# Attention with routed experts on one core: routed rows leave PSUM by VectorE, and a prep of q stands behind the routing step

## The chip, the cores and the metric

The kernel runs on one core of a Trainium2 chip. TensorE (PE) multiplies, its weight loads are listed apart (PEld); VectorE (DVE), ScalarE (ACT) and GpSimd (POOL) compute; SyncE (SP) issues transfers. The metric is the device time of one execution in microseconds (us), lower is better.

## The reference

Attention over 8 batches, 8 heads, 576 positions and 64 dimensions, with a bias from a small network, and then a mixture of 8 experts in which each of the 4608 tokens goes to one expert:

```python
scores = scale * np.matmul(q, k.transpose(0, 1, 3, 2))
...
h = np.maximum(x @ w1 + b1, 0.0)
bias = h @ w2
scores = scores + bias.transpose(2, 0, 1)[None, :, :, :]
scores = scores - np.max(scores, axis=-1, keepdims=True)
attn = np.exp(scores)
attn = attn / (np.sum(attn, axis=-1, keepdims=True) + 1e-09)
return np.matmul(attn, v).astype(np.float32)
...
logits = x @ w_gate + modality_bias[modality_id]
e_idx = np.argmax(logits, axis=1)
...
for e in range(E):
    mask = e_idx == e
    h = np.maximum(x[mask] @ w1[e], 0.0)
    out[mask] = gate_w[mask, None] * (h @ w2[e])
```

Here x is the attention's output with the heads side by side, 4608 rows of 512, and gate_w is the softmax weight of the chosen expert.

## The kernel before, in words

First a table of biases is built (to about 72 us), then attention runs over 32 pairs of heads, n = 0 to 31, four pairs to a batch, and last come expert tiles of 256 routed rows. Attention and the routing of the batch before are interleaved by a list written out by hand, `ORDER` (L572): each pair has five units, u = 0 to 4, and each letter of a unit's string is one operation, emitted in that order. Each engine runs its own instructions in the order in which they were emitted.

The letters that matter here: S is one slot of scores (L415), on TensorE, followed by a reduction on VectorE (L445) that reads PSUM, adds the bias and finds the row's extreme; e and f are the exponentials of the unit's slots on ScalarE (L459). T and t transpose a chunk of exponentials (L473) into the banks eps1 and eps0, from which ScalarE or VectorE copies it to eT. R is rtrans (L495), which transposes the remainders into a bank of xps, copied to rT by ScalarE. The digits 0 to 4 are parts of prep (L368) of the next pair: four transposes into a bank of xps (L379), scaled into QT by VectorE (L319) or copied into KT. W issues the transfers that swap QT's halves. a and b are av (L504), the product with v, through xps as well. X and B take the next step of the routing of the batch before from a list (`route_steps`, L730), if what it needs has been done; D stores finished rows to memory.

Two banks of PSUM, xps0 and xps1, serve all of R, prep, av and the routing steps. `xbank` (L306) hands them out in turn, so each user waits until what was put there two uses before has been copied out. The copies go through `take` (L312), which gives a copy to ScalarE where its name is in `ON_ACT` (L310), and to VectorE otherwise.

A batch's routing steps with kind X are the logits (two parts, L758), their transposes, the ranks (L833), and five row steps (`s_rows`, L854): TensorE transposes 128 tokens of the attention's output back into rows (L859), the rows are copied to one of two buffers (xrb) that take turns, GpSimd scales them (L866), appends the gate (L869), and D stores them (L902). For batches 0 to 6 row steps 0 and 1 fall in unit 4 of the pairs 6, 10, ..., 30, row step 2 in unit 0 of the pairs 7, 11, ..., 31, and steps 3 and 4 in unit 4 of those; the second part of the logits falls in unit 0 of pairs 5, 9, ..., 29. In the other units 0 the X finds nothing to do. The last batch's steps run beside the first expert tiles, and their rows go to buffers in the space of NBm.

```python
def xbank(self):
    self.n_x += 1
    return self.xps[self.n_x % 2]
...
self.take("xr", xr[0:n, 0:DM], ps[0:n, :])
```

Of the kernel before, what the change touches and what calls it, by code (L numbers as in the profile page):

```python
# [22 lines left out]
S = 576  # L23
# [84 lines left out]
class Attn:  # L108
# [198 lines left out]
        self.n_x += 1  # L307
        return self.xps[self.n_x % 2]

    ON_ACT = ("av0", "av1", "e00", "e11", "e21", "e30", "e31", "e40", "e41", "prep2", "prep5", "rT", "xr", "lt0")  # L310

    def take(self, what, out, ps, scale=1.0):  # L312

        if what in self.ON_ACT:
            self.nc.scalar.activation(out, ps, AF.Copy, scale=scale)  # L315
# [213 lines left out]
    def first_steps(self, route):  # L529
# [40 lines left out]


    ORDER = (  # L572
# [893 lines left out]
```

## Time and profile before

| | |
|---|---|
| median of 3 runs | 1157.64 us (1157.51 to 1159.23) |
| profiled execution | 1149.1 us |
| its span, first to last instruction | 1147.3 us |
| TensorE busy | 1098.1 us, 96% of the span |
| VectorE busy | 739.5 us, 64% |
| ScalarE busy | 730.8 us, 64% |
| GpSimd busy | 359.7 us, 31% |
| mean granted TensorE clock | 0.994 |

The time of the profiled execution includes a little before the first and behind the last instruction, 1.8 us together. Rows of the trace hold the start, the duration, the engine, the line, the operation, what it writes and reads, and in brackets how long the engine was idle before it and what ended that. A row with x4 merges four instructions that stand together. TensorE's matmuls overlap, so a row's duration is not the pace of its instructions; the starts of the weight loads show that better.

### The profile page before, as it was taken

What the parts mean: (1) busy time and instruction counts of PE and PEld (TensorE: products, weight loads), DVE (VectorE), ACT (ScalarE), POOL (GpSimd) and SP (SyncE); (2) the same over time, 40 slices, a digit from 0 to 9 for tenths busy, and PEclk for the clock granted to TensorE, in tenths of its full rate; (3) what the DMA queues carried; (4) which work ended last, traced back from release to release, by engine and by line L of the source; (5) the groups of instructions that cost most, each with busy time, mean ns of one, the idle gap of its engine ahead of it and who ended that gap; (6) DMA issues with size and microseconds to landing.
All of it is one profiled execution on the core that took longest, in us unless ns stands there. A gap on an engine that the chain in (4) does not pass through costs nothing. (4 is left out here: it accounts for less than half of the span.)

```text
span 1147.3 us, 22992 instructions
## 1 busy us (share of the span) xinstructions
PE 1098.1 (96%) x8202; PEld 917.0 (80%) x8202; DVE 739.5 (64%) x1548; ACT 730.8 (64%) x1428; POOL 359.7 (31%) x514
## 2 busy tenths in 40 slices
PE   7979999999999999999999899999999999999997
PEld 3458877778788778887777779899998999999975
DVE  8965667676585766766767457675565556645576
ACT  7767767667767767676766666445564555545566
POOL 0013324434435344254443234412112212222121
PEclk9989999999999999999999999999999999999999
DMA  6984434754636445355464611212115115111370
GB/s 175 222 186 110 113 94 121 113 119 109 127 96 132 116 125 115 98 127 116 113 124 108 195 33 66 52 46 65 38 38 194 56 47 203 46 43 60 112 268 22
DMA packets 91456, 124.54 MB, mean 109 GB/s; under 512 B 35713, under 2 KB 60673, under 8 KB 91332
## 3 DMA queue, kind: packets, MB, share of 16 engines
q1 hardware_dynamic: 83236, 101.61, 36.0%
q0 software_dynamic: 8000, 21.35, 6.1%
q8 instruction: 68, 1.11, 0.5%
q14 instruction: 56, 0.46, 0.2%
q10 hardware_dynamic: 96, 0.00, 0.0%
HBM read 140.36 MB, written 19.90 MB: 140 GB/s over the span
## 5 line engine op out<-in xcount | busy, mean ns | idle before, releaser
L459 ACT ACTIVATE Eb<-Eb,mn 128x576 f32<-128x576 f32 x288 | 221.9, 773 | 82.2 <-DVE mn L445 82.1
L445 DVE CUSTOM_DVE_ANT_0 Eb<-sps,NBm 128x576 f32<-128x576 f32 x256 | 185.7, 753 | 104.7 <-ACT eT L315 78.5
L430 PE MATMUL sps<-KT,QT 128*128 128x288 f32 x1152 | 202.7, 310 | 11.5 <-DMA QT<-QT 8.0
L430 PEld LDWEIGHTS sps<-KT,QT 128*128 128x128 f32 x1152 | 160.5, 190 | 21.3 <-issue 7.9
L1181 PE MATMUL p<-QT,w1hi 128*128 128x256 f32 x1152 | 162.1, 283 | 1.6 <-ACT w1hi L1154 1.6
L1181 PEld LDWEIGHTS p<-QT,w1hi 128*128 128x128 f32 x1152 | 149.4, 192 | 3.9 <-ACT w1hi L1154 2.5
L473 PE MATMUL eps<-idf,Eb 128*128 128x128 f32 x1024 | 146.0, 276 | 3.4 <-DVE eT L317 2.9
L1207 POOL DMA_INDIRECT out<-mo,idt x36 | 48.1, 1336 | 297.7 <-ACT mo L1206 261.2
L1184 DVE SCALAR_TENSOR_TENSOR hl<-p,hh 128x512 fp32r<-128x512 f32 x72 | 49.7, 690 | 139.9 <-ACT hh L1183 139.9
L515 PE MATMUL xps<-eT,vraw 128*64 128x288 f32 x1024 | 137.8, 411 | 1.1 <-DVE QT L319 0.5
L464 POOL COPY rem<-Eb 128x128 f32<-128x128 f32 x128 | 37.1, 289 | 302.3 <-ACT Eb L459 301.3
L473 PEld LDWEIGHTS eps<-idf,Eb 128*128 128x128 f32 x1024 | 118.5, 142 | 16.2 <-DVE eT L317 4.9
L315 ACT ACTIVATE eT<-eps 128x512 f32<-128x512 f32 x192 | 110.6, 592 | 32.3 <-PE eps L473 28.5
L1148 DVE TENSOR_TENSOR w2lo<-NBm,w2hi 128x1024 fp32r<-128x1024 f32 x84 | 102.4, 1225 | 24.9 <-ACT w2hi L1147 24.9
L1198 PE MATMUL p<-w2hi,hh 128*128 128x512 f32 x288 | 114.2, 396 | 0.0
L1183 ACT ACTIVATE hh<-p 128x512 fp32r<-128x512 f32 x72 | 43.0, 597 | 110.7 <-PE p L1181 100.4
L1198 PE MATMUL p<-w2hi,hl 128*128 128x512 f32 x288 | 112.5, 391 | 0.0
L317 DVE COPY eT<-eps 128x512 f32<-128x512 f32 x96 | 65.9, 686 | 61.1 <-ACT xTb L315 54.1
L515 PEld LDWEIGHTS xps<-eT,vraw 128*64 128x64 f32 x1024 | 67.9, 136 | 46.0 <-issue 5.3
L1148 DVE TENSOR_TENSOR w1lo<-NBm,w1hi 128x1024 fp32r<-128x1024 f32 x84 | 97.7, 1225 | 0.2 <-ACT w1hi L1147 0.2
L1181 PE MATMUL p<-QT,w1lo 128*128 128x256 f32 x576 | 92.8, 283 | 0.2 <-DVE w1lo L1155 0.2
L1147 ACT CAST w2hi<-NBm 128x1024 fp32r<-128x1024 f32 x84 | 86.8, 1041 | 0.7 <-ACTq L1311 0.7
(233 smaller groups left out, 1907.8 us busy)
## 6 DMA issues: line engine op xcount, KB each, us to landing
NBm<-moe_w SPq DMA_DIRECT2D x24, 2048.0 KB
NBm<-moe_w SPq DMA_DIRECT2D x46, 1024.0 KB
QT<-QT SPq DMA_DIRECT2D x64, 304.0 KB
NBm<-xTb SPq DMA_DIRECT2D x32, 288.0 KB
KH<-KT SPq DMA_DIRECT2D x64, 144.0 KB
qraw<-q SPq DMA_DIRECT2D x32, 256.0 KB
kraw<-k SPq DMA_DIRECT2D x32, 256.0 KB
vraw<-v SPq DMA_DIRECT2D x32, 256.0 KB
```

Of the source, the lines that this page charges most:

```text
L315: self.nc.scalar.activation(out, ps, AF.Copy, scale=scale)
L317: self.nc.vector.tensor_copy(out, ps)
L430: nc.tensor.matmul(ps[:, half, :], q, k[:, HS * half : HS * half + HS], start=i == 0, stop=i == len(terms) - 1, skip_group_check=True,)
L445: nc.vector.tensor_tensor_reduce(out=e.rearrange("p (t w) -> p t w", t=2), in0=ps, in1=nb.rearrange("p (t w) -> p t w", t=2), scale=1.0, s ...
L459: self.nc.scalar.activation(e, e, AF.Exp, bias=mn, scale=-1.0, accum_out=sm)
L473: nc.tensor.transpose(ps[:, k, :], e[:, part, P * k : P * k + P], self.idf)
L515: nc.tensor.matmul(ps[o, :], v[:, h, k, :], self.eT[:, h, k, sl], start=k == 0, stop=False, tile_position=(0, 64 * h), skip_group_check=True,)
L1147: self.nc.scalar.copy(h, w)
L1148: self.nc.vector.tensor_tensor(l, w, h.bitcast(F32), op=ALU.subtract)
L1181: nc.tensor.matmul(ps[:, a, :], w[:, c, fs], x[:, c, :], start=i == 0, stop=i == len(ops) - 1)
L1184: nc.vector.scalar_tensor_tensor(hl[:, sl, :], ps, 0.0, hh[:, sl, :].bitcast(F32), op0=ALU.max, op1=ALU.subtract)
L1198: nc.tensor.matmul(ps, h[:, f, sl], m[:, f, :], start=i == 0, stop=i == len(ops) - 1)
```

## The change

The name xr leaves the list of copies that ScalarE does: the five row copies of each batch, 40 in all, go to VectorE. And in unit 0 the prep part 0 moves from before X to behind f; as e and f are work of ScalarE alone, the prep then stands behind the routing step on TensorE and VectorE.

```diff
-    ON_ACT = ("av0", "av1", "e00", "e11", "e21", "e30", "e31", "e40", "e41", "prep2", "prep5", "rT", "xr", "lt0")
+    ON_ACT = ("av0", "av1", "e00", "e11", "e21", "e30", "e31", "e40", "e41", "prep2", "prep5", "rT", "lt0")
...
-        "S S T t R 0 X e f C Z L",
+        "S S T t R X e f 0 C Z L",
```

On TensorE in unit 0 of pair 15, with row step 2 (L859), prep part 0 (the first L379) and, in unit 1, prep part 1 (the last line); xps_77 and xps_78 are the two banks, and L501 is rtrans:

```order
 L501 MATMUL xps_78<-idf,rem_2_3863 128x128
 L501 MATMUL xps_78<-idf,rem_3_3904 128x128
-L379 MATMUL xps_77<-idr,qs 128x128 x4
-L859 MATMUL xps_78<-idf,xTb_94 128x128 x4
+L859 MATMUL xps_77<-idf,xTb_94 128x128 x4
+L379 MATMUL xps_78<-idr,qs 128x128 x4
 L430 MATMUL sps_736<-KT_108,QT_73 128x288 x4
 L379 MATMUL xps_77<-idr,qs 128x128 x4
```

Row step 2 and prep part 0 change places and banks; prep part 1 keeps its bank, in which row step 2 now stands before it instead of prep part 0.

On VectorE from the end of pair 14 to unit 0 of pair 15; eT<-eps_738 is e20, L847 and L849 belong to the positions, L445 with mn_0 and mn_1 are the reductions of slots 0 and 1, and QT is prep part 0:

```order
 L841 TENSOR_TENSOR rks_3926<-rks_3926,oh 128x40
+L317 COPY xrb_90<-xps_78 128x512
 L317 COPY eT<-eps_738 128x4x128
 L847 TENSOR_REDUCE pf_3948<-rks_3926 128x5
 L849 CAST pos_3950<-pf_3948 128x5
+L317 COPY xrb_89<-xps_77 128x512
 L445 ISA Eb,mn_0_3966<-sps_736,NBm 128x576
 L445 ISA mn_0_3966 128x1
 L445 ISA Eb,mn_1_3972<-sps_737,NBm 128x576
 L445 ISA mn_1_3972 128x1
```

Two row copies enter the queue ahead of the reductions of slots 0 and 1. Right behind these the third one enters, ahead of the scaling of prep part 0:

```order
-L319 TENSOR_SCALAR QT_72<-xps_77 128x512
+L317 COPY xrb_90<-xps_77 128x512
+L319 TENSOR_SCALAR QT_72<-xps_78 128x512
 L445 ISA Eb,mn_2_4018<-sps_736,NBm 128x576
```

It writes the same buffer, xrb_90, as the first of the three.

On TensorE in unit 0 of pair 13, with the second part of the logits (L767):

```order
 L501 MATMUL xps_78<-idf,rem_2_3423 128x128
 L501 MATMUL xps_78<-idf,rem_3_3465 128x128
-L379 MATMUL xps_77<-idr,qs 128x128 x4
-L767 MATMUL xps_78<-xTb_94,wgb 32x64 x4
+L767 MATMUL xps_77<-xTb_94,wgb 32x64 x4
+L379 MATMUL xps_78<-idr,qs 128x128 x4
```

Logits and prep change places and banks in the same way. The orders of GpSimd and SyncE are as before.

## Rows read from the trace of the kernel before

**Rows 1.** The page's totals: busy time of each engine, its share of the span, its instructions.

```profile
PE 1098.1 (96%) x8202; PEld 917.0 (80%) x8202; DVE 739.5 (64%) x1548; ACT 730.8 (64%) x1428; POOL 359.7 (31%) x514
```

**Rows 2.** Busy time of each engine in the attention stretch: the stretch and its length, busy time and instructions of each engine, then the granted clock, the transfers' share and GB/s.

```profile
90.00:670.00 580.00, 560.49 (x4528) 456.98 (x4525) 373.04 (x1006) 406.17 (x979) 240.12 (x390) 1.00 0.52 118
```

**Rows 3.** What TensorE waited for between 88 and 670 us: the line that waited, the releaser, total us, times, longest.

```profile
PE sps L430 <- DMA QT<-QT: 4.8, 4, 2.7
PE xps L767 <- ACT rT L315: 3.5, 7, 0.5
PE sps L430 <- DVE mn L445: 3.2, 8, 0.5
PE xps L859 <- ACT rT L315: 3.0, 6, 0.5
```

**Rows 4.** Two groups of copies out of PSUM over the whole span: busy us, mean ns of one, idle before.

```profile
L317 DVE COPY eT<-eps 128x512 f32<-128x512 f32 x96 | 65.9, 686 | 61.1 <-ACT xTb L315 54.1 <-PE eps L473 5.3 <-PE sps L430 1.4
...
L315 ACT ACTIVATE xrb<-xps 128x512 f32<-128x512 f32 (+1 forms) x42 | 24.3, 594 | 10.7 <-PE xps L379 4.9 <-DMA xg<-xrb 4.3 <-PE sps L430 1.0
```

**Rows 5.** Instructions in order of time, end of pair 14 and begin of pair 15: the copies of row steps 0 and 1 on ScalarE, VectorE's work, the two groups of transposes of unit 0 on TensorE, and the first scaling of rows on GpSimd.

```profile
338.61 0.60 ACT L315 ACTIVATE xrb<-xps 128x512 f32<-128x512 f32 x1
...
339.56 0.68 DVE L317 COPY eT<-eps 128x512 f32<-128x512 f32 x1
...
340.16 0.18 DVE L847 TENSOR_REDUCE pf<-rks 128x5 f32<-128x40 f32 x1
340.34 0.60 ACT L315 ACTIVATE xrb<-xps 128x512 f32<-128x512 f32 x1
340.37 0.75 DVE L849 CAST pos<-pf 128x5 int32<-128x5 f32 x1
...
340.78 1.04 PE L473 MATMUL eps<-idf,Eb 128*128 128x128 f32 x8
341.03 0.74 DVE L445 CUSTOM_DVE_ANT_0 Eb<-sps,NBm 128x576 f32<-128x576 f32 x1
...
341.05 1.04 POOL L866 TENSOR_TENSOR xrb<-xrb,rec 128x512 f32<-128x512 f32 x1
...
341.70 0.75 DVE L445 CUSTOM_DVE_ANT_0 Eb<-sps,NBm 128x576 f32<-128x576 f32 x1
```

**Rows 6.** The same list a little later, units 0 and 1 of pair 15: rtrans (L501), prep part 0 (L379), the stores of rows (SPq L902, issue), rT, row step 2 (L859), scores of slot 2, prep part 1, the copy of row step 2, and the first av (L515).

```profile
341.65 0.60 PE L501 MATMUL xps<-idf,rem 128*128 128x128 f32 x4
...
341.98 0.42 PEld L379 LDWEIGHTS xps<-idr,qs 128*128 128x128 f32 x4
...
342.25 1.47 SPq L902 DMA_DIRECT2D xg<-xrb  x2
342.39 0.60 ACT L315 ACTIVATE rT<-xps 128x512 f32<-128x512 f32 x1
...
343.04 0.66 PE L859 MATMUL xps<-idf,xTb 128*128 128x128 f32 x4 [0.50 <-ACT rT L315]
343.43 0.57 PEld L430 LDWEIGHTS sps<-KT,QT 128*128 128x128 f32 x4
...
343.94 0.44 PEld L379 LDWEIGHTS xps<-idr,qs 128*128 128x128 f32 x4
...
344.38 0.76 DVE L445 CUSTOM_DVE_ANT_0 Eb<-sps,NBm 128x576 f32<-128x576 f32 x1 [1.05 <-PE sps L430]
344.39 0.60 ACT L315 ACTIVATE xrb<-xps 128x512 f32<-128x512 f32 x1 [1.40 <-DMA xg<-xrb]
...
345.07 0.69 DVE L319 TENSOR_SCALAR QT<-xps 128x512 fp32r<-128x512 f32 x1
...
345.67 0.75 DVE L445 CUSTOM_DVE_ANT_0 Eb<-sps,NBm 128x576 f32<-128x576 f32 x1
345.81 1.65 PEld L515 LDWEIGHTS xps<-eT,vraw 128*64 128x64 f32 x16
```

**Rows 7.** Prep part 1 (L379) and the copy of row step 2 in the first and the last of the six pairs 7, 11, 15, 19, 23 and 27, in order of time.

```profile
195.07 0.44 PEld L379 LDWEIGHTS xps<-idr,qs 128*128 128x128 f32 x4
...
195.58 0.60 ACT L315 ACTIVATE xrb<-xps 128x512 f32<-128x512 f32 x1 [1.46 <-DMA xg<-xrb]
...
566.42 0.44 PEld L379 LDWEIGHTS xps<-idr,qs 128*128 128x128 f32 x4
...
567.19 0.60 ACT L315 ACTIVATE xrb<-xps 128x512 f32<-128x512 f32 x1 [1.71 <-PE xps L379]
```

**Rows 8.** Weight loads in order of time: the second part of the logits (L767) and the scores behind it in pair 13, then prep part 0 and the scores behind it in pair 16, where no routing step stands between.

```profile
305.73 0.16 PEld L767 LDWEIGHTS xps<-xTb,wgb 128*32 128x32 f32 x8 [0.64 <-ACT rT L315]
...
305.98 0.56 PEld L430 LDWEIGHTS sps<-KT,QT 128*128 128x128 f32 x4
...
360.60 0.42 PEld L379 LDWEIGHTS xps<-idr,qs 128*128 128x128 f32 x4
360.97 0.56 PEld L430 LDWEIGHTS sps<-KT,QT 128*128 128x128 f32 x4
```

**Rows 9.** The last batch's rows beside an expert tile: splits of the weights on VectorE, and the transposes of row step 3.

```profile
712.10 1.23 DVE L1148 TENSOR_TENSOR w2lo<-NBm,w2hi 128x1024 fp32r<-128x1024 f32 x1 [0.25 <-ACT w2hi L1147]
...
713.52 5.19 DVE L1148 TENSOR_TENSOR w1lo<-NBm,w1hi 128x1024 fp32r<-128x1024 f32 x4 [0.20 <-ACT w1hi L1147]
...
719.37 0.66 PE L859 MATMUL xps<-idf,xTb 128*128 128x128 f32 x4 [2.16 <-DVE QT L1166]
```

## The prediction

> **What bounds the kernel now.** I read the totals first, then the busy time of the attention stretch, then the list of TensorE's waits there, and last the order of time around one place where the change acts. The totals show TensorE busy for 96% of the span, VectorE and ScalarE for 64% each [rows 1]. In the attention stretch, 90 to 670 us, TensorE is busy 560.49 of 580.00 us at a granted clock of 1.00, the 2.4 GHz level, with VectorE at 373.04 and ScalarE at 406.17 [rows 2]. So TensorE sets the pace there, and neither a freed ScalarE nor a fuller VectorE counts unless it moves a TensorE wait. The waits are few: 3.5 us in 7 pieces before the logits (L767) and 3.0 us in 6 pieces before the row transposes (L859), each on the copy of rT by ScalarE; the rest is smaller pieces and transfers of QT [rows 3]. These 13 pieces of 0.50 us stand exactly in the units 0 that the change reorders: the prep of q, then the routing step, which needs the bank that rtrans has just filled.
>
> **The change part by part.** Pair 15 stands for the six places of rows (pairs 7, 11, 15, 19, 23, 27; pair 31 prepares no next pair). The banks alternate: rtrans fills one (I call it B), the next user takes the other (A), the one after that B again.
>
> *Row steps 0 and 1, unit 4 of pairs 6, 10, ...* Their copies leave ScalarE (0.59 us each) and enter VectorE's queue at 0.69 us each, a row of the same shape and kind [rows 4]; one VectorE copy puts the next start back by 0.60 (339.56 to 340.16). Copy 0 takes the start at 339.56, e20 goes to 340.16, the two position steps to 340.76 and 340.97, copy 1 to 341.63 (340.37 to 341.03 is 0.66), and the reduction of slot 0 from 341.03 to 342.23, that of slot 1 from 341.70 to 342.90 [rows 5]. Who waits? The transposes that refill e20's bank are the second half of a group from 340.78 to 341.82, so they start near 341.3, and e20 now ends at 340.85: covered. GpSimd scales row 0 only at 341.05, copy 0 ends at 340.25: covered, and the store of row 0 is issued at 342.25 as now [rows 5, 6]. If that cover were gone, the cost would be up to the 0.60 of a copy for each, 3.6 us over six places. ScalarE's gain is worth nothing: rT starts at 342.39 because rtrans ends at about 342.25, not because ScalarE is busy [rows 6].
>
> *The swap in pair 15.* Now row step 2 comes first. Its bank A is the one of row step 1, whose copy ends on VectorE at 341.63+0.69 = 342.32; with 0.05 to pass on (rT ends at 342.99, its waiter starts at 343.04) the transposes start at 342.37 instead of 343.04 [rows 6]. But prep of q needs bank B, so it is the one that waits for rT until 343.04, and the scores of unit 1 follow 0.37 behind its start (360.60 to 360.97 in a unit without routing step [rows 8]): 343.41, against 343.43 now. The wait of 0.50 is handed on, not removed: 0.0 us. The scores' bank is free by then (slot 0's reduction, 0.74 long, ends at 342.97).
>
> *What becomes late next.* Prep part 1 in unit 1 takes bank A, from which row 2 must be copied. Before the change that bank had held prep part 0, and row 2 lay in B, which is needed only three steps later. Row 2's copy writes the buffer that row 0 is being stored from: ScalarE starts it at 344.39, although its transposes ran from 343.04 to 343.70; the store was issued at 342.25, so it is free 2.14 us after the issue [rows 6]. VectorE will be free at about 343.66, stand before the same store until 344.39, and hand bank A over at 344.39+0.69+0.05 = 345.13. Prep part 1 starts at 343.94 today [rows 6]: 1.19 us late, with nothing else for TensorE to do, since its queue is in program order. In the first of the six places the copy starts 0.51 behind prep part 1, in the last 0.77 [rows 7]; over the six the mean is 0.585. So 6 x (0.585+0.69+0.05) = 7.95 us. From below, if VectorE need not wait for the store: copy at 343.70, bank free at 344.44, 0.50 us each, 3.0 us. From above, if VectorE's lateness is passed on whole (its next four items all stand behind the copy): 1.19+0.7 each, some 11.5. I take 7.95, since all six rows show the copy starting after the transposes by the same margin, and VectorE meets the same store.
>
> The Trainium skill's page "DMA: Bandwidth & Descriptors" (section on the anatomy of one DMA, given for transfers issued by GpSimd) puts a transfer at about 2.0 us fixed plus its bytes over 436 GB/s, and says the fixed part is mostly the confirmation of the write. For 128 rows of 2064 bytes that is an estimate of 2.6 us, against the 2.14 us here; by it each of the six waits would be 0.46 longer and the sum 12.3 instead of 9.5. The trace decides for 2.14, and both speak against placing this copy ahead of what VectorE owes TensorE.
>
> *Behind it.* On VectorE the copy is followed by the scaling of prep 0 (344.99), slot 2's reduction (345.59) and the scaling of prep 1 (346.28 to 346.97; spacings 0.60 and 0.69 from 345.07 to 345.67 and 344.38 to 345.07 [rows 6]). The first av of unit 1 takes that bank; it starts at 345.81 now, 347.00 with the shift, and may start at 347.02. I take 0.05 each, 0.3 us; bounds 0 and 0.35.
>
> *The logits units (pairs 5, 9, ..., 29: seven).* Here too the wait for rT is handed on to the prep. Now the scores follow the logits' start by 0.25 (305.73 to 305.98), then the prep's by 0.37 [rows 8]: 7 x 0.12 = 0.84 us lost. Bounds: 0 to 7 x 0.25.
>
> *Row steps 3 and 4* stand side by side in unit 4 of pairs 7, 11, ... and put two copies before e20. The scores and the first transposes of the next unit lie between them and the next use of their banks and of e20's. I take nothing; where that cover fails it is up to one copy each, 0.60 x 7 = 4.2 us.
>
> *The last batch's five rows* are prepared beside the expert tiles. One TensorE wait there, 2.16 us at 719.37, is on VectorE, which runs four weight splits of 5.19 us from 713.52 right before it [rows 9]; row 2's copy now stands ahead of these splits and puts them back by 0.41, as the split before it ends at about 713.3. 0.41 us; bounds 0 and 3 (five copies, each 0.60).
>
> Sum: 7.95 + 0.3 + 0.84 + 0.41 = 9.5 us. The profiled execution took 1149.1 us (span 1147.3), the median of the runs is 1157.64, 8.5 higher; I add the sum to the median: 1167.1 us.
>
> **The rivals.** *Faster:* the 13 waits of 0.50 us simply go, 6.5 us, 1151.1 us. That needs row 2's copy to be over before prep part 1 comes at 343.94, so the store would have to be done by 343.2, 0.95 us after its issue; and something other than rT's bank for the prep. The rows speak against both. Chance 0.10. *A small loss:* the store does not hold VectorE up (the lower bound): 3.0+0.84+0.41 = 4.3 us, 1161.9 us. For it: ScalarE's late start is put down to TensorE in the last of the six places [rows 7]. Chance 0.08. *No change:* what TensorE loses comes back at waits further down, such as the 4.8 us for QT transfers [rows 3], and the split copy is hidden more than I see: within 2.3 us of 1157.6. Against it: those transfers are issued behind the same preps and move along. Chance 0.07. *A cascade:* VectorE, already late, passes delay on into the next units: 11.5+0.84+0.41 = 12.8 us, 1170.4 us. Against it: VectorE idles 1.05 us before slot 2's reduction [rows 6], and the av of 2 us hides the rest. Chance 0.05.
>
> **How the numbers follow.** The forecast has 0.70. A measurement of this kernel tells about 0.2%, 2.3 us, from no change. Faster: 0.10. Within: 0.07 of the no-change case and 0.02 of the forecast's lower tail, 0.09. Slower: 0.81. The forecast's own range is 1163.5 to 1171; the range given, 1160 to 1172, takes in the small loss and the cascade and leaves out the first and third rival.
>
> **What would show it.** Right: no wait of row transposes or logits on rT, but waits of the preps (L379) in units 0 of the same pairs on rT; in unit 1 of pairs 7, 11, ... prep part 1 waiting some 1.2 us on VectorE, whose copy of row 2 waits for the store; six times. The reductions of slot 0 behind two row copies start about 1.2 us later without a TensorE wait. Wrong: prep part 1 without a wait, a copy that starts straight behind its transposes, or new waits in the transposes that follow e20.

## The result, and the profile after

The change makes the kernel slower: 1164.61 us (median of 7 runs, 1161.85 to 1167.86) against 1153.05 us for the kernel before on the same chip (7 runs, 1145.91 to 1159.23). The ratio is 1.0097 with a 95% interval of 1.0072 to 1.0123, that is 11.2 us of 1153, between 8.3 and 14.2. The forecast was a loss of 9.5 us. The profiled execution of the new kernel took 1161.85 us, its span is 1159.7.

First the totals and the attention stretch of the changed kernel, the views of [rows 1] and [rows 2]; the stretch is 10 us longer here, because attention ends later.

```profile
PE 1102.8 (95%) x8202; PEld 917.6 (79%) x8202; DVE 759.5 (65%) x1588; ACT 713.2 (62%) x1388; POOL 360.0 (31%) x514
```

```profile
90.00:680.00 590.00, 563.16 (x4523) 456.75 (x4519) 390.20 (x1041) 391.18 (x943) 239.67 (x390) 1.00 0.49 116
```

VectorE has 40 instructions more and 20.0 us more work, ScalarE 40 fewer and 17.6 us less. The instruction counts of TensorE are the same and its granted clock in the stretch is 1.00 as before, the 2.4 GHz level. What has grown is TensorE's idle time in the stretch: 19.5 us of 580 before, 26.8 us of 590 now. The list of its waits between 88 and 685 us says which waits these are, the view of [rows 3].

```profile
PE xps L379 <- DVE xrb L317: 6.4, 6, 1.2
PE xps L379 <- ACT rT L315: 5.9, 13, 0.5
PE sps L430 <- DMA QT<-QT: 4.3, 3, 2.9
PE sps L430 <- DVE mn L445: 3.8, 9, 0.6
...
PE xps L515 <- DVE QT L319: 2.7, 2, 1.9
```

The logits (L767) and the row transposes (L859) no longer wait for rT. The prep of q (L379) waits for it in their place, in the same 13 units: 5.9 us, against 3.5 and 3.0 in [rows 3]. And the first line is new: six waits of a prep for a bank that VectorE's copy of a row (xrb, L317) still holds. The weight loads of the same matmuls come earlier in TensorE's queue and show more of each wait:

```profile
PEld xps L379 <- ACT rT L315: 8.5, 13, 0.7
PEld xps L379 <- DVE xrb L317: 7.8, 6, 1.4
```

Six waits, 7.8 us, 1.3 each. Pair 15 of the changed kernel in order of time, the place of [rows 5] and [rows 6]:

```profile
344.27 0.68 DVE L317 COPY xrb<-xps 128x512 f32<-128x512 f32 x1
...
345.76 0.68 DVE L317 COPY xrb<-xps 128x512 f32<-128x512 f32 x1
...
346.81 0.60 PE L859 MATMUL xps<-idf,xTb 128*128 128x128 f32 x4
...
346.97 1.48 SPq L902 DMA_DIRECT2D xg<-xrb  x2
...
347.11 0.60 ACT L315 ACTIVATE rT<-xps 128x512 f32<-128x512 f32 x1
...
347.76 0.39 PEld L379 LDWEIGHTS xps<-idr,qs 128*128 128x128 f32 x4 [0.59 <-ACT rT L315]
...
348.10 0.56 PEld L430 LDWEIGHTS sps<-KT,QT 128*128 128x128 f32 x4
...
349.13 0.69 DVE L317 COPY xrb<-xps 128x512 f32<-128x512 f32 x1 [1.33 <-DMA xg<-xrb]
349.74 0.68 DVE L319 TENSOR_SCALAR QT<-xps 128x512 fp32r<-128x512 f32 x1
349.88 0.40 PEld L379 LDWEIGHTS xps<-idr,qs 128*128 128x128 f32 x4 [1.22 <-DVE xrb L317]
...
351.75 1.65 PEld L515 LDWEIGHTS xps<-eT,vraw 128*64 128x64 f32 x16
```

Read it backwards from the first av (L515) at 351.75. Prep part 1 starts at 349.88, 1.22 us after TensorE was ready for it, because the copy of row step 2 has to empty its bank. That copy starts only at 349.13, although its transposes began at 346.81: it writes the buffer from which row 0 is being stored, and VectorE stood 1.33 us before that store. The store was issued at 346.97, 2.16 us before the copy. All this stands 4.72 us later than in [rows 6] by rT (342.39 there, 347.11 here); the copy by 4.74, the av by 5.94. So the unit is 1.22 us longer, all of it at this one wait.

The length of a batch shows the same without any list. One wait of TensorE comes back once in each batch of four pairs: the one for VectorE's minimum, 0.4 us long, before the scores (L430). From one such wait to the next, in batches without a wait for a transfer, first before and then after the change:

```profile
250.00 0.80 PE L430 MATMUL sps<-KT,QT 128*128 128x288 f32 x4 [0.40 <-DVE mn L445]
...
323.80 0.81 PE L430 MATMUL sps<-KT,QT 128*128 128x288 f32 x4 [0.41 <-DVE mn L445]
```

```profile
404.39 0.80 PE L430 MATMUL sps<-KT,QT 128*128 128x288 f32 x4 [0.41 <-DVE mn L445]
...
479.66 0.81 PE L430 MATMUL sps<-KT,QT 128*128 128x288 f32 x4 [0.39 <-DVE mn L445]
```

73.80 us before, 75.27 after: 1.47 us for each batch. The forecast's terms give 7.95/6 = 1.33 for prep part 1, 0.05 for the av and 0.12 for the logits, together 1.50. I use this batch length below: in most batches without other waits it repeats within about 0.05 us, where whole runs scatter by 6 to 13 us. It is not the same everywhere: another batch before the change (397.59 to 471.76) takes 74.17, because there the av in pair 19 waits 0.39 us for the scaling of prep part 1; against that one the difference is 1.10.

Last, the expert tile of [rows 9], the first row transposes behind the four splits:

```profile
730.00 0.66 PE L859 MATMUL xps<-idf,xTb 128*128 128x128 f32 x4 [2.70 <-DVE QT L1166]
```

2.70 us against 2.16: 0.54 lost, where 0.41 was forecast. Behind this wait the granted clock differs too, three microseconds of each kernel in the view of [rows 2], first after the change and then before:

```profile
731.50:734.50 3.00, 3.00 (x9) 2.33 (x8) 0.00 (x0) 0.00 (x0) 2.19 (x3) 0.50 0.28 105
```

```profile
720.87:723.87 3.00, 3.00 (x15) 2.47 (x14) 0.00 (x0) 0.00 (x0) 2.12 (x3) 1.00 0.24 88
```

The changed kernel ran there at 0.50, the 1.2 GHz level, and the kernel before at 1.00. From these row transposes to the next weight loads of L1181 it took 7.38 us (729.99 to 737.37) instead of 5.75 (719.37 to 725.12): 1.6 us that the forecast did not have.

### The profile page after: what moved, and what is told of

It reads as the page before. It is cut to its first block, busy times and chain, and to the rows that moved or that the text cites. A ratio compares the mean times of both kernels' runs of the same rounds, so it can differ in the third digit from the quotient of the medians.

```text
span 1159.7 us, 22983 instructions
## 1 busy us (share of the span) xinstructions
PE 1102.8 (95%) x8202; PEld 917.6 (79%) x8202; DVE 759.5 (65%) x1588; ACT 713.2 (62%) x1388; POOL 360.0 (31%) x514
## 5 line engine op out<-in xcount | busy, mean ns | idle before, releaser
L445 DVE CUSTOM_DVE_ANT_0 Eb<-sps,NBm 128x576 f32<-128x576 f32 x256 | 185.6, 752 | 90.8 <-ACT eT L315 75.2
L430 PE MATMUL sps<-KT,QT 128*128 128x288 f32 x1152 | 202.2, 310 | 11.7 <-DMA QT<-QT 7.6
L430 PEld LDWEIGHTS sps<-KT,QT 128*128 128x128 f32 x1152 | 160.2, 189 | 20.9 <-issue 8.8
L1181 PE MATMUL p<-QT,w1hi 128*128 128x256 f32 x1152 | 162.1, 283 | 1.6 <-ACT w1hi L1154 1.6
L1181 PEld LDWEIGHTS p<-QT,w1hi 128*128 128x128 f32 x1152 | 149.4, 192 | 3.9 <-ACT w1hi L1154 2.5
L473 PE MATMUL eps<-idf,Eb 128*128 128x128 f32 x1024 | 146.3, 276 | 2.9 <-DVE eT L317 2.8
L515 PE MATMUL xps<-eT,vraw 128*64 128x288 f32 x1024 | 137.8, 411 | 3.3 <-DVE QT L319 2.7
L473 PEld LDWEIGHTS eps<-idf,Eb 128*128 128x128 f32 x1024 | 118.9, 142 | 15.5 <-DVE eT L317 5.2
L515 PEld LDWEIGHTS xps<-eT,vraw 128*64 128x64 f32 x1024 | 67.8, 136 | 48.6 <-issue 5.4
L317 DVE COPY eT<-eps 128x512 f32<-128x512 f32 x96 | 65.7, 685 | 54.9 <-ACT xTb L315 54.3
L1181 PE MATMUL p<-QT,w1lo 128*128 128x256 f32 x576 | 92.8, 283 | 0.2 <-DVE w1lo L1155 0.2
```

The costliest lines, as they stand in the source:

```text
L317: self.nc.vector.tensor_copy(out, ps)
L430: nc.tensor.matmul(ps[:, half, :], q, k[:, HS * half : HS * half + HS], start=i == 0, stop=i == len(terms) - 1, skip_group_check=True,)
L445: nc.vector.tensor_tensor_reduce(out=e.rearrange("p (t w) -> p t w", t=2), in0=ps, in1=nb.rearrange("p (t w) -> p t w", t=2), scale=1.0, s ...
L473: nc.tensor.transpose(ps[:, k, :], e[:, part, P * k : P * k + P], self.idf)
L515: nc.tensor.matmul(ps[o, :], v[:, h, k, :], self.eT[:, h, k, sl], start=k == 0, stop=False, tile_position=(0, 64 * h), skip_group_check=True,)
L1181: nc.tensor.matmul(ps[:, a, :], w[:, c, fs], x[:, c, :], start=i == 0, stop=i == len(ops) - 1)
```

## The experiments

Theory T is the forecast's: TensorE runs its queue in program order, and with row step 2 ahead of prep part 0, prep part 1 gets the bank of row step 2, whose copy waits for the store of row 0; the engine that makes this copy does not matter. The rival V says that VectorE's 27 us of added copies (40 of 0.68 us each; its busy time grew by 20.0) make it late for what TensorE waits on. The first four runs tell these apart; the others ask whether the same reading finds a faster order. Each ratio is to the kernel before on the same chip. All nine kernels compute the whole reference.

**The two parts alone.** One kernel has only the copies on VectorE, the other only the new order.

```diff
 e1_copy_only
-    ON_ACT = (..., "rT", "xr", "lt0")
+    ON_ACT = (..., "rT", "lt0")
 e2_order_only
-        "S S T t R 0 X e f C Z L",
+        "S S T t R X e f 0 C Z L",
```

> Only the row copies go to VectorE, the order of units stays as before. Theory T (the loss comes from bank A: with the new order row step 2 holds it, and its copy waits for the store of row 0, so that prep part 1 waits): row step 2 is in bank B again, so prep part 1 finds A free but for the scaling of prep part 0, which stands behind two row copies: about 0.4 us at prep part 1 and 0.2 us at the first av, in six pairs, plus 0.4 us beside the expert tiles: +4.2 us, ratio 1.0036. The 13 waits of 0.50 us for rT at row step 2 and the logits stay. Theory V (the load of 40 more copies on VectorE costs the time, whatever the order): the whole loss, +11 us, ratio 1.009 or more.

> Only the prep moves behind the routing step, the row copies stay on ScalarE. Theory T: ScalarE's copy of row 2 starts behind the store as before and takes 0.60 us instead of 0.69, so prep part 1 waits for it six times, 0.585+0.60+0.05 = 1.2 us by the starts of the weight loads: 7.4 us, with 0.84 us in the seven logits units +8.2 us, ratio 1.007, and nothing beside the expert tiles. Theory V: VectorE has no more work than before, so no loss, or a gain of up to 6.5 us from the 13 waits, ratio 0.994 to 1.000.

Measured: the copies alone 1.0070 (1.0043 to 1.0096), the order alone 1.0074 (1.0046 to 1.0102). The order alone, with every copy still on ScalarE, waits at the same places for nearly the same time:

```profile
PE xps L379 <- ACT xrb L315: 6.1, 6, 1.2
PE xps L379 <- ACT rT L315: 5.8, 13, 0.5
```

In its pair 15 ScalarE stands before the store as VectorE does in the whole change:

```profile
352.04 1.47 SPq L902 DMA_DIRECT2D xg<-xrb  x2
...
354.19 0.60 ACT L315 ACTIVATE xrb<-xps 128x512 f32<-128x512 f32 x1 [1.41 <-DMA xg<-xrb]
```

So the six waits need no load on VectorE. The batch of this run takes 75.03 us (408.95 to 483.98), 1.23 more than before.

The copies alone lose by another way than the whole change, and by more than I had expected: 1.0070 lies between the 1.0036 of T and the 1.009 of V, so by its time alone this run decides nothing. The order of time in its pair 15 (347.9 to 350.4 us):

```profile
347.98 0.46 PE L379 MATMUL xps<-idr,qs 128*128 128x128 f32 x4
348.33 0.69 DVE L317 COPY xrb<-xps 128x512 f32<-128x512 f32 x1 [0.74 <-DMA xg<-xrb]
348.94 0.75 DVE L445 CUSTOM_DVE_ANT_0 Eb<-sps,NBm 128x576 f32<-128x576 f32 x1
349.61 0.69 DVE L319 TENSOR_SCALAR QT<-xps 128x512 fp32r<-128x512 f32 x1
350.21 0.75 DVE L445 CUSTOM_DVE_ANT_0 Eb<-sps,NBm 128x576 f32<-128x576 f32 x1
350.35 1.65 PEld L515 LDWEIGHTS xps<-eT,vraw 128*64 128x64 f32 x16 [0.68 <-DVE QT L319]
```

Prep part 1 comes without a wait here, before the row copy has even begun, but VectorE stands before the store and then has a reduction and the scaling of prep 1 behind it. The av needs that scaling's bank and waits 0.68 us here by the weight loads, 0.54 by the matmuls. TensorE's list has 4.3 us in 7 such waits, six of them at these places. The batch is 0.81 longer than before (480.77 to 555.38 is 74.61). So a copy on VectorE can cost time too, here through the same store. In the whole change this av wait is not added on top: prep part 1 is already 1.22 late there and the copy hides in that. By batches 0.81 and 1.23 make 1.47, and by runs 0.70% and 0.74% make 0.97%, not 1.44%.

**A third buffer for the rows.** The whole change, but row 2 gets a buffer of its own, so its copy has no store to wait for. The room comes from raw q, kept once instead of twice. The control is the kernel before with the same two buffer edits.

```diff
-        self.xrb = [cp.tile([P, XW], F32, name=f"xrb{k}") for k in range(2)]
+        self.xrb = [cp.tile([P, XW], F32, name=f"xrb{k}") for k in range(3)]
...
-            t = self.raw.tile([P, 9, D], F32, tag=nm + "raw", name=f"{nm}raw{n}")
+            t = self.raw.tile([P, 9, D], F32, tag=nm + "raw", name=f"{nm}raw{n}", bufs=1 if nm == "q" else 2)
...
```

> The whole change with a third row buffer, so that the copy of row 2 need not wait for the store of row 0 (room for it comes from one instead of two buffers for the raw q, which are read and loaded at least 7 us apart). Theory T: the copy starts straight behind VectorE's reduction of slot 1, some 0.7 us earlier; prep part 1 waits about 0.4 us instead of 1.0; 2.8+0.84+0.41 = +4.0 us, ratio 1.0035. If the store were not what holds the copy, or if VectorE's load costs the time (V): as the whole change, +11 us.

> The kernel before with the third row buffer and the single buffer for raw q alone, as a control for the runs that use them. Both theories: nothing on TensorE's waits, a batch without transfer waits takes 73.8 us as before, ratio 1.000; if the buffers themselves gain or lose, the other runs have to be read against this one.

Measured: the change with the third buffer 1.0029 (1.0002 to 1.0056), the control 0.9994 (0.9970 to 1.0017). In pair 15 of the former:

```profile
345.46 1.47 SPq L902 DMA_DIRECT2D xg<-xrb  x2
...
346.21 0.69 DVE L317 COPY xrb<-xps 128x512 f32<-128x512 f32 x1
346.26 0.39 PEld L379 LDWEIGHTS xps<-idr,qs 128*128 128x128 f32 x4 [0.59 <-ACT rT L315]
...
347.11 0.45 PEld L379 LDWEIGHTS xps<-idr,qs 128*128 128x128 f32 x4
```

Row 2's copy starts 0.75 us after the issue of row 0's store instead of 2.16, and prep part 1 follows with no wait. The six waits are gone from the list; the 13 waits on rT stay (5.9 us). The batch is 73.95 (402.07 to 476.02), 0.15 over before and 0.06 over the 73.89 of the control (476.73 to 550.62). This is also what rules V out: all 40 copies are still on VectorE here, and the batch hardly grows. Together with the run of the order alone it shows T: the six waits need the order and the shared buffer, and neither the engine of the copy nor VectorE's load. The expectation had left 0.4 us at each prep part 1; there is none. What is left is of the size of the logits unit, which is 0.09 us longer (see below). Six such batches, a seventh logits unit and 0.54 in the expert tile make 1.0 to 1.5 us; the runs say 3.3, with an interval from 0.2 to 6.5.

**An order that removes the waits.** If prep part 0 keeps its place and the routing step goes behind the next scores, in unit 1, rT has time to be written: its waits should go, not be handed on. One kernel does only this; another adds the third buffer and gives row 2's copy alone to VectorE.

```diff
 e7_x_behind_scores_plain
-        "S S T t R 0 X e f C Z L",
-        "S 1 t e S 4 f T a B W D C",
+        "S S T t R 0 e f C Z L",
+        "S X 1 t e S 4 f T a B W D C",
 e4_x_behind_scores (the same order, three row buffers, one raw q)
-    ON_ACT = (..., "rT", "xr", "lt0")
+    ON_ACT = (..., "rT", "xr0", "xr1", "xr3", "xr4", "lt0")
...
-                self.take("xr", xr[0:n, 0:DM], ps[0:n, :])
+                self.take(f"xr{c}", xr[0:n, 0:DM], ps[0:n, :])
```

> Only the order: the routing step behind the first scores of unit 1, all row copies on ScalarE, two buffers. Theory T: the seven waits of 0.50 us before the logits go; before row step 2 they go too, but its copy on ScalarE now stands behind two exponentials and holds the bank that prep part 4 needs, until about 345.3 in the time of pair 15, where TensorE comes at 344.7: about 0.6 us wait in six places. Together -3.5-3.0+3.6 = -3 us, ratio 0.9975, and a batch without transfer waits takes 73.4 us against 72.9 with the third buffer. Rival: the buffer does not matter, -6 us, 72.9 us.

> A version meant to take the waits for rT away: the routing step moves from unit 0 to unit 1, behind the scores of its first slot, so that the scores stand between rtrans and the next user of its bank; prep part 0 stays where it was. The third row buffer as in the run beside it; the copy of row step 2 alone goes to VectorE, where it stands behind the reduction of slot 2. Theory T (a wait is only removed if something that needs no bank of xps fills the time): the 13 waits of 0.50 us go, nothing waits in their place: -6 us, ratio 0.995. Theory V: five copies fewer on VectorE than in the change, so a small loss or nothing; no gain, since waits for a bank come back elsewhere: ratio 1.000 or more.

Measured: 0.9951 (0.9922 to 0.9979) for the plain order, 0.9977 (0.9953 to 1.0001) with buffer and copy. No wait on rT is left in either. Their batches are 73.09 us (400.70 to 473.79 in the plain one) and 72.85, 0.7 and 0.95 shorter than before. The plain order did better than expected (0.9975, 73.4 us): of the 3.6 us of waits that were to come back at the copy of row 2, only 0.6 us in 3 pieces are in its list. The other did worse in its runs (0.995 expected): its batch is shorter, yet it is no faster than the first as far as the runs can tell. Its profiled execution shows why that may be: it waits 11.4 us in 4 pieces for the transfers of the swap, where before waited 4.8 [rows 3]. What SyncE issues around the first av of unit 1 in pair 15 of that kernel:

```profile
348.99 1.65 PEld L515 LDWEIGHTS xps<-eT,vraw 128*64 128x64 f32 x16
...
350.04 0.57 SPq L333 DMA_DIRECT2D kraw<-k  x1
350.67 1.12 SPq L339 DMA_DIRECT2D kraw<-k  x2
351.89 3.75 SPq L403 DMA_DIRECT2D QT<-QT  x1
...
357.13 0.48 SPq L404 DMA_DIRECT2D QT<-QT  x1
```

The two transfers of the swap (L403, L404) are issued behind the loads of raw k for two pairs ahead, and one issue takes 3.75 us. This pair shows the order on the queue and not a loss: no wait for a swap follows it. The four waits end at 232.18, 381.56, 603.22 and 644.00, and the issues of the swaps before them took 0.5 to 0.6 us each.

**The raw loads of k behind the swap.** The load of raw k is not needed for a whole pair; it moves behind the swap, in unit 1. This was run with the last kernel's order, with the kernel before, and with the change.

```diff
-        "S X 1 t e S 4 f T a B W D C",
+        "S X 1 t e S 4 f T a B W M D C",
...
+                            if op == "L":
+                                loads = self.qk_loads(n + 2)
+                                for _ in range(3):
+                                    next(loads)
+                            elif op == "M":
+                                for _ in loads:
+                                    pass
...
```

> The version with the routing step behind the scores, and in it the loads of raw k moved from unit 0 to behind the swap of QT's halves in unit 1. In the profiles so far TensorE waits 4 to 11 us in all for that swap, and SyncE issues it behind six loads, some of which take 2 to 4 us to issue. If that queue makes the swap late: the waits for QT fall from 11 us to under 3 us, and the ratio to about 0.990. If the transfer itself is late (its engines are full), nothing changes: ratio 0.998 as without it.

> The kernel before with the loads of raw k behind the swap, as in the fastest version. If the swap's place in SyncE's queue caused the waits for QT, they fall from 4.8 to under 3 us here, nearly all of it in pair 31, and the runs scatter less; ratio about 0.995. The 13 waits of 0.50 us for rT stay, a batch takes 73.8 us.

> The whole change with the loads of raw k behind the swap: change against no change with the transfer waits out of the way. Theory T: seven batches of about 1.4 us and 0.5 us beside the expert tiles, so 10 to 11 us above the run beside it, ratio about 1.004 to 1.005 to the kernel before; six waits of 1.0 us of prep part 1 on the copy of row 2. Rival (part of the loss lies in the swap's transfers, which come later in the change): under 6 us above it, ratio 1.000 or less.

Measured with the new order: 1141.62 us, ratio 0.9890 (0.9862 to 0.9918), all six runs between 1140.40 and 1142.97. This is 1.1% faster than the kernel before, with an interval from 0.8 to 1.4%. SyncE's issues in its pair 15:

```profile
341.30 1.65 PEld L515 LDWEIGHTS xps<-eT,vraw 128*64 128x64 f32 x16
...
342.33 0.54 SPq L403 DMA_DIRECT2D QT<-QT  x1
342.93 0.58 SPq L404 DMA_DIRECT2D QT<-QT  x1
343.56 3.66 SPq L333 DMA_DIRECT2D kraw<-k  x1
```

The swap is issued 1.0 us after the start of the av instead of 2.9, and the slow issue now falls on a load that TensorE does not wait for. Only one wait for a swap is left in the stretch (2.5 us instead of 11.4); the batch is 72.86 us (319.73 to 392.59), as without the late loads. So the gain lies in the waits for the swap. Whether the swap comes sooner because its issue stands earlier or because less traffic is ahead of it, the run does not tell.

The other two are a miss and half a miss. With the order before, late loads give 0.9989 (0.9967 to 1.0010) where I expected a gain of 0.5%: a wait of 2.9 us for QT remained, and one of 2.7 for QD. Ahead of the first stands an issue of the swap itself that took 3.14 us (215.78), so late loads do not always keep the swap off a slow issue. With the change they give 1.0025 (1.0006 to 1.0044), 4.5 us over their own control, not the 10 to 11 expected. The six waits are all there (6.4 us on the row copy, 5.9 on rT), and later in the stretch it loses as T says: 402.01 to 477.31 is 75.30, against 74.15 (400.66 to 474.81) and 73.82 (474.81 to 548.63) in its control. But in the batch that ends near 250 us it is 3.5 us shorter than its control:

```profile
172.52 0.79 PE L430 MATMUL sps<-KT,QT 128*128 128x288 f32 x4 [0.40 <-DVE mn L445]
...
252.39 0.81 PE L430 MATMUL sps<-KT,QT 128*128 128x288 f32 x4 [0.41 <-DVE mn L445]
```

```profile
172.89 0.80 PE L430 MATMUL sps<-KT,QT 128*128 128x288 f32 x4 [0.40 <-DVE mn L445]
...
249.25 0.80 PE L430 MATMUL sps<-KT,QT 128*128 128x288 f32 x4 [1.46 <-DVE mn L445]
```

The control has a wait of 2.88 us for a swap in that batch (at 229.69), and behind it the granted clock is 0.50 from 230 to 233 us; the changed kernel with late loads has neither there. So with this order of loads a part of the loss comes back at transfers, in which the forecast's third rival is partly right; whether the later preps cause that, or the swap merely meets other traffic, these two profiles do not settle.

## Why the prediction was right

*The waits on rT are handed on, not removed: 0.0.* Right. All 13 are on prep part 0 now, in the same units; the scores come 0.34 behind its start (347.76 to 348.10), 0.37 forecast. At the six places of rows they start 0.99 to 1.00 us after rT's copy does, 1.04 to 1.05 before. The rival that gave 6.5 us back needed them gone; they went only when the routing step was moved behind the next scores.

*Prep part 1, 6 x 1.33 = 7.95 us.* Right in mechanism and size: 1.22 in pair 15 for 1.19, 7.8 by the weight loads for all six. The choice between the bounds was decided by the store: VectorE meets it exactly where ScalarE did, 2.16 us after the issue here for 2.14 in [rows 6], and with ScalarE copying in the run of the order alone it is 2.15 (352.04 to 354.19). The lower bound, 0.50 each, for a copy that need not wait, was itself too high: with the third buffer VectorE takes the copy before the scaling of prep 0, is through by 346.90, and prep part 1 loads at 347.11 without a wait. The forecast had VectorE free some 0.7 us too late there, which the store covered. The cascade of 11.5 did not come.

The Trainium skill's page "DMA: Bandwidth & Descriptors", section on the anatomy of one DMA, would have put the store at an estimated 2.6 us, by a fit given for transfers that GpSimd issues; the 2.14 to 2.17 measured from issue to the next write in these runs decide for the smaller value, for transfers that SyncE issues.

*The av behind it, 0.3 us.* Smaller: at the six places it is 0. In pair 15 it starts 4.64 us behind rT, 3.42 before: 1.22, which is the wait of prep part 1 alone. In pair 19 a wait of 0.39 us that the av had before is gone. The two av waits in the list are elsewhere (below). From rT to this av the six places together take 28.3 us now and 20.8 before: 7.5 us, for the 8.25 forecast up to here.

*The logits, 0.84 us.* Somewhat smaller: in six of the seven units the weight loads of the scores start 0.99 to 1.00 us after rT's copy does, 0.90 to 0.91 before. That is 0.09 each for the 0.12 forecast, 0.6 us for seven. In the seventh (pair 29) a wait for VectorE's minimum comes on top, as it does in the buffer control.

*Row steps 0, 1, 3 and 4, 0.0.* Right: the transposes that follow e20 (L473) wait 2.8 us in 9 pieces, 2.9 in 9 before. A detail was off: slot 0's reduction behind the two copies was to come some 1.2 us later and came 0.62 later (1.36 us ahead of rT's copy in [rows 5, 6], 0.74 now), since the cast between the copies took 0.17 us for the 0.75 of [rows 5]. It was covered either way.

*The expert tile, 0.41 us.* Measured 0.54, and 0.54 too in the runs where only the copies had moved (2.70 for 2.16), with nothing in the run of the order alone (2.15). The 1.6 us at the lower clock behind it were not forecast.

*The sum, 9.5 us.* Term by term the profiled executions give 7.5 + 0.6 + 0.54 = 8.7. By batches it is 6 x 1.47 = 8.8, the logits unit of the seventh 0.09 and the tile 0.54, which makes 9.5; with 1.10 a batch it is 7.2. The runs say 11.2, from 8.3 to 14.2. What they have above the forecast, 1.7 us, is less than the interval's half width, and no run shows where it lies; the clock is a candidate, as told at the end. On the base it went the other way: the median of before was 1157.64 in three runs and 1153.05 in seven, so the time forecast, 1167.1, is 2.5 us too high while the difference is 1.7 too low. That the two errors offset each other in part is luck; the terms of the mechanism are not.

## What to carry to other kernels

When an order of work is changed to spare a wait, follow each PSUM bank to the instruction that will empty it, and from there to what that instruction itself waits for: here a store of another row, two steps away, made over 80% of the loss by batches. A wait for a result goes only if other work is put between producer and consumer; swapping two consumers of the same rotating banks hands it on. And measure such changes on a stretch that repeats beside the whole time, which scatters by several us: here a batch, good to 0.05 us where no other wait falls into it.

## What was not expected

**An issue on SyncE can take several us.** In the pair shown above one issue took 3.75 us, its neighbours 0.5 to 1.1; with the loads moved the slow one (3.66) is still there, on another transfer. Among the issues that stand as rows of their own between 88 and 690 us, some 300 in each profile, 3 to 5 take 2 us or more, on whatever transfer, up to 5.99 for a load of raw q in the run with the third buffer. That a slow issue of the swap costs time is not shown, since the waits of 11.4 us stand behind quick ones. What is shown is that with the new order the late loads are worth 0.9%: they made six runs of 1140.4 to 1143.0, where the same kernel with the loads in their old place scattered from 1145.2 to 1158.4 (12 runs, on another chip). With the order before, the same edit also narrowed the scatter, to 1149.2 to 1153.6 in 12 runs against 1144.9 to 1161.2 in 23, without moving the median by more than can be told.

**The granted clock has a share in the times.** In every one of these kernels the longer runs tend to have the lower mean granted clock: the changed kernel's seven go from 1161.85 us at 0.992 to 1167.86 at 0.986. In the profiles TensorE falls to the 1.2 GHz level for some 3 us right behind single waits, as in the expert tile above: it did so behind 5 of the 6 waits of 2.7 us at that place in the eleven profiles, and behind 2 of the 5 of 2.15. It also did so behind two of the 18 waits on the row copy, in the run of the order alone (0.50 from 279 to 282 us) and in the change with late loads (0.50 from 272 to 275). So a wait can cost more than its length. The forecast had no term for this; whether the change brings the clock down more often than the kernel before, these profiles, one for each kernel, do not settle.

**One stall without a visible cause.** In pair 13 of the changed kernel, where there is no row step, both copying engines stand still until 312.33 us:

```profile
309.00 0.69 DVE L319 TENSOR_SCALAR QT<-xps 128x512 fp32r<-128x512 f32 x1 [0.81 <-DMA KH<-KT]
...
312.33 0.69 DVE L319 TENSOR_SCALAR QT<-xps 128x512 fp32r<-128x512 f32 x1 [1.90 <-PE eps L484]
312.39 0.60 ACT L315 ACTIVATE eT<-eps 128x512 f32<-128x512 f32 x1 [2.56 <-PE eps L484]
...
313.08 2.16 PE L515 MATMUL xps<-eT,vraw 128*64 128x288 f32 x16 [1.88 <-DVE QT L319]
```

The av pays 1.88 us for it. The releaser named is a group of transposes of TensorE; it may as well be a transfer that the view does not show. It is a single event of one execution, and no run was made on it; it stays open. A smaller wait of the av (0.82) stands in pair 29, where six of the other profiles have one too (0.35 to 1.17).
